# Whole first K load and fewer, larger pieces of the output projection in a decode-attention kernel bound by its load stream

## The chip, the cores and the metric

The kernel runs on one core of a Trainium2 chip. The metric is the device time of one execution in microseconds (us), lower is better. Where I say "span" I mean the time from the first to the last recorded instruction of one execution; it is about 1.4 to 2.0 us shorter than the device time, and it can be compared with positions in the trace.

Engines in the profile: PE is the matmul engine, PEld its weight load, DVE the vector engine, ACT the scalar engine, SP the engine that issues the large loads ("SPq" is its sequencer).

## The reference, cut to what matters

```python
def _A_ref(x, k_cache, v_cache, wq, wo):          # x: one token of 512; 32 heads of 128; 16384 keys
    q = (x @ wq) ...
    scores = jnp.einsum('bhqd,bhkd->bhqk', q, k_cache) * Dh ** (-0.5)
    p = _softmax(scores, axis=-1)
    o = jnp.einsum('bhqk,bhkd->bhqd', p, v_cache)
    return o... @ wo                              # wo: 4096 x 512
...                                               # _B_ref: a small gated MLP
g = _sigmoid((x * gate_w).sum(-1, keepdims=True))
return g * a + (1 - g) * b
```

K and V are 128 MB each in bf16 and are read once. Everything else is small: 4 MB each of `wq` and `wo`, under 3 MB of MLP weights.

## The kernel before

K and V are read in 16 pairs of heads. A load of one pair's K or V is 8 MB: 128 partitions, one row of 64 KB in each. Three such buffers rotate. Loads go out on the SP queue in the order K0, K1, V0, K2, V1, K3 and so on, and each waits until the user of its buffer is done. In particular V1 (the "second V") goes into the buffer of K1, so its issue waits until the scores of pair 1 are finished.

The last load is `wo`, 32 rows of 1 KB per partition, in six pieces. The first 24 rows are multiplied "the wide way" (eight products at a time into four column groups of the array), the rest row by row, two products each.

```python
K_CUTS = (0, 128, 256)
V_CUTS = (0, 160, 224, 256)
WO_CUTS = (0, 16, 24, 28, 30, 31, 32)
WIDE = 24
...
for n, kind, i in loads:
    wait = [user[n - 3]] if n >= 3 else [w_free] if buf[n % 3] is setup else []
    src = (k_src if kind == "k" else v_src)[i]
    cuts, sems = (0, KP), [(ld_k if kind == "k" else ld_v)[i % 2]]
    if n == 0:
        cuts, sems = K_CUTS, ld_kf                    # first K: two halves, two semaphores
    elif i == NP - 1:
        cuts, sems = (K_CUTS, ld_kh) if kind == "k" else (V_CUTS, ld_vp)
    for a, b, done in zip(cuts[:-1], cuts[1:], sems):
        sp.op(lambda e, ...: e.dma_start(out=buf[n % 3][:, a * Dh:b * Dh], ...), wait=..., inc=(done, 16))
...                                                   # (cut)
def warm(e, n, again=False): ...                      # filler products: 128 columns of weights, 512 wide
def fill(e, m): ...                                   # filler product: m columns, no weight load
...                                                   # (cut) the tail, after the last V:
def pe_wide(e):
    va, pa = (counter(e, n, 0) for n in ("wa", "oa"))
    warm(e, 1)
    with e.Fori(0, WIDE // WG) as t:
        ...                                           # eight wide products
        fill(e, 1)
...
w_ok = act.op(lambda e: e.copy(out=d_sb[:, :], in_=d_ps), wait=[(pe.sem, pe.n)], mark=True)
...
for j, (a, b) in enumerate(zip(WO_CUTS[:-1], WO_CUTS[1:])):
    for k in range(max(a, WIDE), b):
        y_ok = add(o2[:, k:k + 1], wo[:, k * D:(k + 1) * D],
                   [(ld_o[j], 16)] if k == a else (), k == H - 1)
    if b == 28:
        add(ones_f[:, 0:1], d_sb[:, :], [w_ok])       # the sums of the wide products
```

The softmax here doesn't subtract the row's maximum and nothing guards it: scores larger than these inputs give would overflow.

## Time and profile before

| | before |
|---|---|
| device time, median of 3 runs | 652.03 us (651.73 to 652.14) |
| span of the profiled execution | 650.5 us |
| bytes loaded | 279.58 MB |
| load queue's share of 16 DMA engines | 99.6% |
| busy PE, DVE, ACT | 66%, 52%, 7% |
| last landing of a `wo` piece (landing records) | 648.53 us |
| from the last landing to the end of the span | 2.00 us |

The first fence is from the page of the profiled execution before. The DMA row has one digit per fortieth of the span, in tenths of busy time (9 is 90% or more). The last line is the chain of waits that ended last.

```profile
span 650.5 us, 7753 instructions
...
PE 428.0 (66%) x2462; PEld 45.7 (7%) x1320; DVE 336.0 (52%) x159; ACT 45.8 (7%) x112; POOL 2.1 (0%) x10
...
DMA  9999999999999999999899999999998999999898
...
q1 hardware_dynamic: 6482, 279.58, 99.6%
...
DMA bufs<-in_A_wo_dram 4%; PE ps_all L719 0%; SPq L645 0%; DVE res L734 0%; ACT p_t L592 0%; ACTq L592 0%; ACTq L612 0%
```

No engine but DMA is near its limit, and the chain ends in the loads of `wo`. So the kernel takes as long as its load stream, plus a short tail.

The next fence is the timeline before, SP and DVE at the start. Columns: start in us, duration in us, engine, line, operation, number of merged instructions, and in brackets how long the engine had been idle and what ended that. L640 on SPq is a K or V load being issued.

```profile
31.83 8.76 DVE L579 TENSOR_TENSOR bufs<-bufs,qb  x2 [0.42 <-DVEq L86]
...
35.27 0.33 SPq L640 DMA_DIRECT2D bufs<-in_A_v_cache_dram  x1
...
59.87 0.33 SPq L640 DMA_DIRECT2D bufs<-in_A_k_cache_dram  x1
...
85.32 0.33 SPq L640 DMA_DIRECT2D bufs<-in_A_v_cache_dram  x1
...
96.69 8.76 DVE L579 TENSOR_TENSOR bufs<-bufs,qb  x2 [12.02 <-DVEq L86]
```

DVE starts on the first K at 31.8 us; V1 is issued at 85.32; DVE waits 12 us for the third K to land at about 96.4.

And the tail before, PE from the last wide group on:

```profile
646.05 0.60 PE L106 MATMUL ps_all<-bufs,o 128*1 x8 [0.72 <-PEq L86]
646.49 0.38 PE L91 MATMUL ps_all<-zero,ident 128*1 128x512 bf16 x1
646.71 0.58 ACT L714 COPY d_sb<-ps_all 128x512 f32<-128x512 f32 x1 [6.01 <-PE ps_all L106]
...
647.20 0.60 PE L719 MATMUL ps_all<-bufs,o 128*1 128x256 bf16 x8 [0.33 <-DMA bufs<-in_A_wo_dram]
...
647.63 0.60 PE L719 MATMUL ps_all<-d_sb,const-float32-1.0 128*1 128x256 f32 x4
...
648.07 0.78 PE L719 MATMUL ps_all<-bufs,o 128*1 128x256 bf16 x8
648.57 0.08 PEld L719 LDWEIGHTS ps_all<-bufs,o 128*1 128x1 bf16 x2 [0.25 <-DMA bufs<-in_A_wo_dram]
648.91 0.36 ACT L734 CAST res<-ps_all 1x256 bf16<-1x256 f32 x1 [1.62 <-PE ps_all L719]
```

The last two weight loads of PE (648.57) wait for a landing, not for PE. The wide sums (the f32 products at 647.63) stand inside the last 1.3 us of PE's work, which ends at 648.89.

### The profile page before, as it was taken

What the parts mean: (1) busy time and instruction counts of PE and PEld (TensorE: products, weight loads), DVE (VectorE), ACT (ScalarE), POOL (GpSimd) and SP (SyncE); (2) the same over time, 40 slices, a digit from 0 to 9 for tenths busy, and PEclk for the clock granted to TensorE, in tenths of its full rate; (3) what the DMA queues carried; (4) which work ended last, traced back from release to release, by engine and by line L of the source; (5) the groups of instructions that cost most, each with busy time, mean ns of one, the idle gap of its engine ahead of it and who ended that gap; (6) DMA issues with size and microseconds to landing.
All of it is one profiled execution on the core that took longest, in us unless ns stands there. A gap on an engine that the chain in (4) does not pass through costs nothing. (4 is left out here: it accounts for less than half of the span.)

```text
span 650.5 us, 7753 instructions
## 1 busy us (share of the span) xinstructions
PE 428.0 (66%) x2462; PEld 45.7 (7%) x1320; DVE 336.0 (52%) x159; ACT 45.8 (7%) x112; POOL 2.1 (0%) x10
## 2 busy tenths in 40 slices
PE   0576866847487574757857476585747757478766
PEld 0000010000101000010000101000010100101012
DVE  3587708356281745618265370835629075465600
ACT  2201010000001000010100001000010100001011
POOL 1000000000000000000000000000000000000000
PEclk9978797969779696987969798686988968798999
DMA  9999999999999999999899999999998999999898
GB/s 387 449 429 451 443 395 451 451 387 451 451 439 399 451 451 415 423 451 451 387 451 451 435 403 451 451 391 447 451 451 387 451 451 431 407 419 484 387 433 342
DMA packets 6491, 279.60 MB, mean 430 GB/s; under 512 B 727, under 2 KB 986, under 8 KB 1370
## 3 DMA queue, kind: packets, MB, share of 16 engines
q1 hardware_dynamic: 6482, 279.58, 99.6%
q8 instruction: 1, 0.02, 0.0%
q10 hardware_dynamic: 8, 0.00, 0.0%
HBM read 279.58 MB, written 0.00 MB: 430 GB/s over the span
## 5 line engine op out<-in xcount | busy, mean ns | idle before, releaser
L579 DVE TENSOR_TENSOR bufs<-bufs,qb x64 | 281.4, 4418 | 168.6 <-DVEq L86 168.6
L91 PE MATMUL ps_all<-bufs,ident 128*128 x960 | 265.0, 432 | 0.0
L496 PE MATMUL ps_all<-bufs,ident 128*128 x64 | 28.4, 444 | 150.8 <-PEq L86 150.8
L106 PE MATMUL ps_all<-bufs,p_t 128*8 x1024 | 79.1, 384 | 30.6 <-PEq L86 19.9
L564 DVE TENSOR_REDUCE s_sb<-ps_all 128x64 f32<-128x512 f32 x64 | 44.0, 688 | 97.4 <-DVEq L86 97.4
L91 PE MATMUL ps_all<-zero,ident 128*8 128x512 bf16 (+1 forms) x147 | 56.4, 384 | 0.0
L592 ACT ACTIVATE p_t<-s_sb 64x256 f32 (+1 forms) x32 | 13.3, 414 | 440.2 <-ACTq L86 439.8
L496 PEld LDWEIGHTS ps_all<-bufs,ident 128*128 128x128 bf16 x64 | 6.3, 99 | 368.0 <-issue 368.0
L106 PEld LDWEIGHTS ps_all<-bufs,p_t 128*8 x1024 | 17.8, 82 | 163.7 <-issue 163.3
L531 PE MATMUL ps_all<-pick,d_sb 128*128 128x2 f32 x128 | 16.8, 253 | 14.8 <-PEq L86 14.8
L531 PEld LDWEIGHTS ps_all<-pick,d_sb 128*128 128x128 f32 x128 | 15.5, 191 | 22.9 <-issue 22.9
L601 ACT COPY d_sb<-ps_all 128x512 f32<-128x512 f32 x16 | 9.4, 585 | 104.3 <-ACTq L86 104.3
L606 ACT CAST ps_all<-zero 128x512 f32<-128x512 bf16 x15 | 8.8, 589 | 1.7
L478 PE MATMUL ps_all<-zero,ident 128*128 128x512 bf16 x18 | 7.0, 389 | 0.0
L669 DVE RECIPROCAL rl<-ps_all 128x32 f32<-128x32 f32 x1 | 0.4, 358 | 11.2 <-PE ps_all L552 11.2
L672 DVE TENSOR_TENSOR o_sb<-ps_all,rl 128x32 bf16<-128x32 f32 x1 | 0.2, 193 | 11.5 <-PE ps_all L531 11.5
L382 DVE TENSOR_TENSOR bufs<-ps_all,ident 128x896 f32<-128x896 f32 x2 | 2.1, 1085 | 7.7 <-PE ps_all L91 7.7
L592 ACT ACTIVATION_READ_ACCUMULATOR p_t<-s_sb (+1 forms) x32 | 5.9, 185 | 0.0
L322 PE MATMUL ps_all<-xgw,const-float32-1.0 1*128 1x3 f32 x2 | 0.6, 358 | 8.0 <-DVE xgw L318 8.0
L106 PE MATMUL ps_all<-bufs,u 128*1 x14 | 2.6, 372 | 3.3 <-ACT ps_all L428 2.5
L91 PE MATMUL ps_all<-bufs,xb 128*128 x12 | 4.4, 491 | 0.0
L346 PE MATMUL ps_all<-bufs,xb 128*128 x4 | 2.1, 517 | 3.2 <-DMA bufs<-in_B_w_in_dram 3.2
(76 smaller groups left out, 42.8 us busy)
## 6 DMA issues: line engine op xcount, KB each, us to landing
bufs<-in_A_k_cache_dram SPq DMA_DIRECT2D x4, 4096.0 KB, 33.2
bufs<-in_A_v_cache_dram SPq DMA_DIRECT2D x1, 5120.0 KB, 33.9
bufs<-in_A_wq_dram SPq DMA_DIRECT2D x1, 4096.0 KB, 12.2
bufs<-in_A_v_cache_dram SPq DMA_DIRECT2D x1, 2048.0 KB, 38.4
bufs<-in_A_wo_dram SPq DMA_DIRECT2D x1, 2048.0 KB, 24.4
bufs<-in_B_w_in_dram SPq DMA_DIRECT2D x1, 1792.0 KB, 15.4
bufs<-in_A_v_cache_dram SPq DMA_DIRECT2D x1, 1024.0 KB, 40.4
bufs<-in_A_wo_dram SPq DMA_DIRECT2D x1, 1024.0 KB, 26.6
```

The source lines that it names most:

```text
L91: ins = eng.matmul(out, lhsT=lhsT, rhs=rhs, **flags).ins
L106: ins = eng.matmul(bank[0:m, 0:n], lhsT=lhsT, rhs=rhs, **flags).ins
L346: if n else matmul_on(nc, e, lambda: e.matmul(args[0], lhsT=args[1], rhs=args[2], **flags), [at, (xa, 0)]))
L382: dve.op(lambda e, h=h, zh=zh: e.tensor_tensor(out=zm[:, 2 * h * ZB:2 * (h + 1) * ZB].rearrange("p (b m k) -> p b m k", b=2, k=FhC), in0=z ...
L478: e.matmul(args[0], lhsT=args[1], rhs=args[2], **flags)
L496: matmul_on(nc, e, lambda: e.matmul(s3, lhsT=ident[:, :], rhs=k3[:, :, 0:W], start=True, **flags), [(kw, 0)])
L531: ins = e.matmul(o2, lhsT=d_sb[:, r * Dh:(r + 1) * Dh], rhs=pick[:, r * 2:(r + 1) * 2], start=False, stop=False, skip_group_check=True)
L564: return e.tensor_reduce(out=s_sb[:, c * QK:(c + 1) * QK], in_=s_ps[c % 2].rearrange("p (j w) -> p j w", w=W), axis=AX.X, op=ALU.add)
L579: e.tensor_tensor(out=k3, in0=k3, in1=qi, op=ALU.mult).then_inc(mul_s, 1)
L592: e.activation(out=p_t[rows, bass.ds(at, NG * 8)].rearrange("p (t c) -> p t c", c=8)[:, :, 4 * s:4 * s + 4], in_=s_sb[rows, :].rearrange(" ...
L601: return e.copy(out=d_sb[:, :], in_=d_ps)
L606: e.copy(out=d_ps, in_=zero[:, :]).then_inc(drn_s, 1)
```

## The change

Its intent: fewer and larger transfers (first K in one load; `wo` in four pieces instead of six), the sums of the wide products moved out of the last microsecond by making only 16 rows wide, and changed filler products on PE.

```diff
-WO_CUTS = (0, 16, 24, 28, 30, 31, 32)
-WIDE = 24
+WO_CUTS = (0, 16, 27, 31, 32)
+WIDE = 16
...
-    ld_kf = [sem(f"ld_kf{b}") for b in range(len(K_CUTS) - 1)]
...
-        warm(e, 2)                       # after each V
+        fill(e, 8, 2)
...
-        if n == 0:
-            cuts, sems = K_CUTS, ld_kf
-        elif i == NP - 1:
+        if i == NP - 1:
...
-        for j in range(len(ld_kf)):
-            hand(e, ld_kf[j], k_s, 1)
+        hand(e, ld_k[0], k_s, 2)
...
-    pe.raw(lambda e: warm(e, 1))         # ahead of the transpose of o
+    pe.raw(lambda e: warm(e, 2))
...
-        warm(e, 1)                       # ahead of the wide products
+        warm(e, 2)
...
+    pe.raw(lambda e: fill(e, 1))
+    add(ones_f[:, 0:1], d_sb[:, :], [w_ok])
     for j, (a, b) in enumerate(zip(WO_CUTS[:-1], WO_CUTS[1:])):
...
-        if b == 28:
-            add(ones_f[:, 0:1], d_sb[:, :], [w_ok])
```

(The rest of the diff only gives `fill` a count and drops an unused argument of `warm`.)

More of the change, by code (lines that the diff above doesn't have):

```diff
@@ L468, in v_buffer, with warm @@
         e.reg_alu(reg, reg, 3, ALU.python_mod)
-    def warm(e, n, again=False):
+    def warm(e, n):
         for j in range(n):
@@ L474, in warm @@
             flags = dict(start=True, stop=True, skip_group_check=True)
-            if j or again:
+            if j:
                 matmul_again(nc, e, *args, **flags)
@@ L478, in warm, with fill @@
                 e.matmul(args[0], lhsT=args[1], rhs=args[2], **flags)
-    def fill(e, m):
-        matmul_again(nc, e, m_ps[0][96:96 + m, :], ident[:, 0:m], zero[:, :], start=True, stop=True,
-                     skip_group_check=True)
+    def fill(e, m, n=1):
+        for _ in range(n):
+            matmul_again(nc, e, m_ps[0][96:96 + m, :], ident[:, 0:m], zero[:, :], start=True,
+                         stop=True, skip_group_check=True)
     def scores(e, i, ka, kw):
```

## The prediction

> **What bounds the kernel.** The load stream. The DMA queue view gives 99.6% of 16 engines' span to queue 1 (279.58 MB). In the transfer records the 16 engines start 1.0 us into the span and never idle until the last piece of the output projection; a 64 KB transfer takes 2.42 us, so 16 engines move 16 x 65,536 B / 2.42 us = 433 GB/s. [...] PE (66%), DVE (52%) and ACT (7%) have slack, and the chain of waits ends in the output-projection loads. So what can change the time is the cost per transfer, and the 2.0 us between the last landing (648.53) and the end (650.5).
>
> **Cost per transfer.** Records by size: 64 KB 2,420 ns, 32 KB 1,213, 16 KB 615, 8 KB 313, 4 KB 160, 2 KB 84, 1 KB 46. A line through the ends gives 37.7 ns per KB plus 8 ns per transfer. Each DMA also writes one semaphore record per engine, 9 ns. An engine carries 8 of the 128 rows.
>
> - First K whole: 8 x (2 x 1,213 - 2,420) + 9 = about 0.06 us saved.
> - Projection pieces: 16, 8, 4, 2, 1, 1 rows cost each engine 8 x (615+313+160+84+46+46) = 10.11 us; 16, 11, 4, 1 cost 8 x (615+423+160+46) = 9.95 us (423 estimated from the line). With two semaphore writes fewer: 0.18 us saved.
>
> The last landing comes 0.24 us earlier, about 648.3.
>
> **First K and DVE.** The halves land at 28.3 and 38.0; DVE starts at 31.8 (held by the gMLP, not by K). Whole, DVE starts at about 38.1, 6.3 us later. The third K then issues at about 66 instead of 59.9, the second V at about 92 instead of 85.3. The stream is queued to about 77 and 97 at those moments, so it never starves. In the timeline DVE idles 12.0 us before the third K (96.7), which absorbs the 6.3. Cost: none.
>
> **The tail on PE.** Wide products of 16 rows take 2 groups of 0.91 us from the landing at 643.3, to about 645.3; ACT copy 0.58, sums 0.36 as today: done by 646.5, before the 11 rows land (about 646.65). The sums thus leave the last microsecond, where they stand today (647.53 to 647.89). Four rows take 0.43 us today, so 11 need 1.18, from 646.7 to 647.9; the next 4 land at about 647.95 and need 0.43, to 648.42; the last row lands at about 648.3. PE thus starts the last two products at 648.42 instead of 648.57: a gain of 0.15 us. The extra filler products only keep PE busy; the granted clock is 1.00 from 636 on (stretches view), and I expect it to stay so.
>
> **Prediction.** 652.03 less 0.15 to 0.24 = 651.85 us. Range 651.4 to 652.3, mostly run-to-run spread (0.4 us among three runs). Faster by over 2%: 0.003; within 2%: 0.994; slower: 0.003.
>
> **What would show it.** DVE's first product at 38; third K issued near 66 with the DMA row still full; sums before the 11 rows; last landing 648.3; the last two products waiting on PE, not on a landing.
>
> **What would make it wrong.** The granted clock falling to 0.5 in the tail: 30 products for 15 rows would take 3.2 us against 1.7 us of landings, up to 1.2 us lost. The stream running dry when the third K or second V issues late: each us is lost whole. More slow transfers (about 0.3 us per engine is lost at 60 to 70 us today) [...]: some tenths either way.

(Two passages are cut: a figure set beside the 433 GB/s that no trace here shows, and a conjecture on what would slow transfers down. Neither was a term of the sum, which came to 0.15 to 0.24 us.)

## The result, and the profile after

A ratio here is the mean time of one kernel's fast runs over that of the other's of the same rounds, so it is not quite the ratio of the medians that are quoted.

The first six runs after: median 652.43 us (651.67 to 652.80), six of before 651.76 (651.71 to 652.14); ratio 1.0007, interval 0.9994 to 1.002: the same. I ran the unedited changed kernel twice more. All 16 runs after, on three occasions: median 652.09, mean 652.13, from 651.62 to 652.80. All 32 fast runs of before: median 651.86, mean 651.91, from 651.66 to 652.42. (One run of before took 957 us and is left out as slow.) In spans: mean 650.52 after (16 runs), 650.43 before (26 runs). So the change gained nothing; if anything it cost 0.1 to 0.2 us (most of that comes from the first six runs; on the two later occasions the means lie 0.05 and 0.14 us above those of before), and its single runs reach 651.4 in span where those of before end at 650.7.

The profiled execution after was one of the fastest. Its page:

```profile
span 650.1 us, 7742 instructions
...
PE 428.8 (66%) x2472; PEld 45.2 (7%) x1312; DVE 336.1 (52%) x159; ACT 45.8 (7%) x112; POOL 2.1 (0%) x10
...
DMA  9999989999999999999999989999998999999898
...
q1 hardware_dynamic: 6050, 279.58, 99.6%
...
PE ps_all L716 0%; PE ps_all L106 0%; PE ps_all L531 0%; PE ps_all L91 0%; PE ps_all L477 0%; ACT d_sb L711 0%; DVE res L731 0%; PE ps_all L677 0%; PE ps_all L673 0%; DVE oT L674 0%
```

432 packets fewer, the same bytes, and the chain that ended last is now made of PE products, no longer of `wo` loads.

The timeline after, SP and DVE at the start:

```profile
34.80 0.33 SPq L638 DMA_DIRECT2D bufs<-in_A_v_cache_dram  x1
38.34 8.76 DVE L579 TENSOR_TENSOR bufs<-bufs,qb  x2 [7.41 <-DVEq L86]
...
66.04 0.33 SPq L638 DMA_DIRECT2D bufs<-in_A_k_cache_dram  x1
...
91.31 0.33 SPq L638 DMA_DIRECT2D bufs<-in_A_v_cache_dram  x1
...
96.39 8.76 DVE L579 TENSOR_TENSOR bufs<-bufs,qb  x2 [5.73 <-DVEq L86]
```

DVE starts 6.5 us later, and so V1 is issued 6.0 us later. DVE still arrives early at the third K (5.7 us of idle time left of 12.0). The tail after:

```profile
645.90 0.60 PE L716 MATMUL ps_all<-d_sb,const-float32-1.0 128*1 128x256 f32 x4 [0.24 <-ACT d_sb L711]
646.45 1.07 PEld L716 LDWEIGHTS ps_all<-bufs,o 128*1 128x1 bf16 x22 [0.46 <-DMA bufs<-in_A_wo_dram]
...
647.75 0.42 PEld L716 LDWEIGHTS ps_all<-bufs,o 128*1 128x1 bf16 x10 [0.23 <-DMA bufs<-in_A_wo_dram]
648.53 0.36 ACT L731 CAST res<-ps_all 1x256 bf16<-1x256 f32 x1 [2.68 <-PE ps_all L716]
```

The sums now stand ahead of the 11 rows. The last 10 weight loads run without a gap after the landing of the 4 rows at 647.71; the last row landed meanwhile, at 647.99. So PE is what ends the tail.

I also worked with three quantities that I computed from the trace's records of single transfers and landings, not from a view of the profile:

- **Work per engine**: the number of transfers of each size times their usual duration (64 KB 2,420 ns, 32 KB 1,213, 16 KB 615, 11 KB 427, and so on), over 16. Before 646.51 us, after 646.31 us: 0.20 us less. This is the forecast's own sum, with the measured 427 ns for an 11 KB transfer where the prediction had estimated 423; it is bookkeeping and not a measurement of time.
- **Last landing**, and the mean of the 16 landings (one per DMA engine) of that last piece.
- **Tail**: span (from the trace, to the nanosecond) minus last landing.

```
kernel       V1 issued  longest extra of   last landing     tail   half-clock stretch
             (us)       a transfer then    last / mean      (us)   after 640 us
                        (94-98.5 us, ns)   of 16 (us)
before        85.32           4            648.53 / 648.38  2.00   none
b_cold        85.64          54            648.47 / 648.13  3.11   644.3 to the end
b_tail        85.97           7            648.15 / 647.90  2.22   642.7 to 646.2
a_khalf       84.81           7            648.17 / 647.92  2.12   none
b_kwhole      91.36         132            648.77 / 648.47  2.00   643.3 to 646.7
after         91.31           8            647.99 / 647.80  2.16   641.0 to 644.4
after_again   90.64           6            647.96 / 647.77  2.09   none
after_third   90.77          11            648.20 / 647.94  2.45   643.6 to 647.0
a_warm        91.21           9            648.22 / 647.84  2.26   643.1 to 646.5
a_cold        91.64         222            648.14 / 647.90  2.96   641.4 to 648.2
a_pieces      91.76         425            648.32 / 647.98  2.00   none
a_hot         92.18        1221            648.69 / 647.90  2.15   none
a_sums        92.28        1338            648.92 / 648.14  2.49   none
a_k32         93.10           6            650.66 / 650.23  2.44   646.0 to 649.4
```

This table holds one traced execution of each kernel (names are explained below; `a_` is an edit of the changed kernel, `b_` of the kernel before). "Longest extra" is how much the slowest 64 KB transfer that began between 94 and 98.5 us took over 2,420 ns; that is where the first transfers of V1 stand (in a_k32, whose stream runs 2.4 us later, they stand 2.4 us later, and there too nothing took over 10 ns longer).

### The profile page after: what moved, and what is told of

Same layout as the page of the kernel before. It is cut to its first block, busy times and chain, and to the rows that moved or that the text cites. A ratio compares the mean times of both kernels' runs of the same rounds, so it can differ in the third digit from the quotient of the medians.

```text
span 650.1 us, 7742 instructions
## 1 busy us (share of the span) xinstructions
PE 428.8 (66%) x2472; PEld 45.2 (7%) x1312; DVE 336.1 (52%) x159; ACT 45.8 (7%) x112; POOL 2.1 (0%) x10
## 3 DMA queue, kind: packets, MB, share of 16 engines
q1 hardware_dynamic: 6050, 279.58, 99.6%
## 5 line engine op out<-in xcount | busy, mean ns | idle before, releaser
L91 PE MATMUL ps_all<-zero,ident 128*8 128x512 bf16 (+1 forms) x165 | 58.2, 385 | 0.0
```

Of the source, the lines that this page charges most:

```text
L91: ins = eng.matmul(out, lhsT=lhsT, rhs=rhs, **flags).ins
```

## The experiments

Theories at the outset. *Clock*: in some executions the array's clock is halved for 3.4 us in the tail, and the change has put more products there. In the clock records of the traces of before and after the granted clock is 1.0 or 0.5 throughout, and the stretches at 0.5 last 3.4 us or more (3.4 to 13.7 us before, 3.4 to 17.1 after). Most half-clock stretches listed above last 3.4 us; that of a_cold lasts 6.8, and that of b_cold from 644.3 us to the end. *Stream*: the whole first K moves DVE's work and disturbs the load stream. *Spread*: there is no difference. Twelve runs, all with five rounds, all correct.

### after_again: the changed kernel unedited

> The changed kernel once more, unedited, for a second trace and five more times. Clock theory (in some executions a 3.4 us half-clock stretch falls on PE's products in the last 6 us, and the change has put more of them there): median 652.2 to 652.6, with single runs spread over 651.6 to 652.9, and whichever profile is slow shows half clock between 644 and 649 us and a gap of over 1 us between last landing and end of the products. Stream theory (the later DVE work after the whole first K makes more slow transfers): same median, but a slow profile shows its last landing after 648.5. Spread theory (no real difference): median within 0.2 of before.

Measured: 652.01 us (651.81 to 652.21) against 651.89 for before on the same chip; ratio 1.0002 (0.9988 to 1.0015). The median is within 0.2 of before's, so this set speaks for *spread*. The profile is a fast one: no half clock from 636.7 us to the end of the products, tail 2.09.

### a_warm: the fillers after each V put back

```diff
-        fill(e, 8, 2)
+        warm(e, 2)
```

> The changed kernel with the two 8-column filler products after each V put back to two 128-column ones. Clock theory, if these fillers are what lets the clock fall in the tail: median near 651.6, spread under 0.5, profile at full clock from 644 to 649. Clock theory, if the fillers do not matter: like the changed kernel, 652.4. Stream theory: like the changed kernel, 652.4.

Measured: 652.25 us (652.00 to 652.70), ratio 1.0006. The profile has a half-clock stretch from 643.1 to 646.5 us although the fillers are the old ones. So the old fillers did not keep the clock up in this trace either. The stretch cost something: the tail is 2.26 us against 2.09 in after_again.

### b_kwhole: before, with only the first K whole

```diff
-    ld_kf = [sem(f"ld_kf{b}") for b in range(len(K_CUTS) - 1)]
...
-        if n == 0:
-            cuts, sems = K_CUTS, ld_kf
-        elif i == NP - 1:
+        if i == NP - 1:
...
-        for j in range(len(ld_kf)):
-            hand(e, ld_kf[j], k_s, 1)
+        hand(e, ld_k[0], k_s, 2)
```

> The kernel before with only the first K made whole. Clock theory: 0.06 us under before, 651.7, spread as before. Stream theory: 652.4 with the wide spread of the changed kernel, and slow transfers in the first 130 us of its trace in place of those at 60 to 90 us.

Measured: 652.07 us (651.84 to 652.19), ratio 1.0001. Neither the 652.4 nor the wide spread of the stream theory. Its trace has several bursts in which most engines' transfers take 0.1 to 0.2 us longer (at 66, 76, 96, 115 and 134 us). The trace of before has such bursts too (66, 86, 144 us), that of a_khalf has none, so they are not the work of the first K. I could not find their cause.

### a_khalf: the changed kernel with the first K in halves

The edit is the reverse of that of b_kwhole, on the changed kernel.

> The changed kernel with the first K in halves again. Clock theory: as the changed kernel, 652.4 with single runs from 651.6 to 652.9. Stream theory: 0.2 us under before, 651.6, narrow spread.

Measured: 651.89 us (651.70 to 652.40), exactly the median of before on that chip; spans 650.3 to 650.6. Not the wide spread that the clock theory asked for, and not a gain of 0.2 us either. Neither theory is settled by these four.

### a_k32: the first K in 32 pieces

```diff
+    ld_kf = [sem(f"ld_kf{b}") for b in range(32)]
...
-        if i == NP - 1:
+        if n == 0:
+            cuts, sems = range(0, KP + 1, KP // 32), ld_kf
+        elif i == NP - 1:
...
-        hand(e, ld_k[0], k_s, 2)
+        for j in range(31):
+            take(e, ld_kf[j], 16)
+        hand(e, ld_kf[31], k_s, 2)
```

> The changed kernel with the first K in 32 pieces of 8 rows, 2 KB per partition. Overhead theory (the stream is busy without a gap, so each transfer's fixed cost goes one to one into the time): 8 x (32 x 84 - 2,420) ns + 31 x 9 ns = 2.4 us on each engine, so last landing near 650.4, span 652.6, time 654.3. Rival (small transfers hide behind something else, so the transfer count does not matter): time as the changed kernel, 652.1, last landing 648.0.

Measured: 654.52 us (654.24 to 654.84), ratio 1.0040 (1.0026 to 1.0054). That is 2.4 us over the 652.09 of the changed kernel, and 2.4 was forecast; the last landing came at 650.66 us, 2.7 us after that of after_again. The landing records show where: K1, the next load after the first K, landed at 59.8 us against 57.4 in after and 57.3 in after_again, and the loads stayed 2.4 to 2.5 us later up to 621 us; the rest of the 2.7 came after that, when the spread of the 16 landings grew from 0.50 to 0.76 us. So more transfers do lengthen the stream, by about the forecast sum, here magnified ten times. The exact hit is partly luck: the 2 KB transfers of this trace took 87 ns in the median and not 84, which would have made the sum 3.2 us.

### a_cold: the changed kernel without fillers in the tail

```diff
-    pe.raw(lambda e: warm(e, 2))
...
-    pe.raw(lambda e: warm(e, 1))
...
-        warm(e, 2)
         with e.Fori(0, WIDE // WG) as t:
...
-            fill(e, 1)
...
-    pe.raw(lambda e: fill(e, 1))
```

> The changed kernel without any filler product after the last V. Clock theory: the granted clock falls to 0.5 in part of 640 to 649 us in most executions, PE ends up to 1.6 us after the last landing instead of 0.47, so time 652.5 to 653.6, with a spread over 0.8. Rival (the tail's clock does not matter, the stream alone sets the end): 652.1, narrow.

Measured: 653.44 us (652.51 to 653.91), ratio 1.0024. The stretches view of a_cold, with one line per stretch of 3 us; after the busy times of PE, PEld, DVE, ACT and POOL come the granted clock, the DMA share and GB/s:

```profile
640.00:643.00 3.00, 1.62 (x13) 1.25 (x13) 0.59 (x3) 0.46 (x1) 0.00 (x0) 0.74 0.94 398
643.00:646.00 3.00, 1.95 (x18) 0.29 (x20) 0.00 (x0) 0.58 (x1) 0.00 (x0) 0.50 0.99 414
646.00:649.00 3.00, 3.00 (x32) 1.70 (x34) 0.00 (x0) 0.00 (x0) 0.00 (x0) 0.63 0.48 182
```

and its timeline in the tail:

```profile
646.78 2.63 PE L712 MATMUL ps_all<-bufs,o 128*1 128x256 bf16 x32
649.48 0.36 ACT L726 CAST res<-ps_all 1x256 bf16<-1x256 f32 x1 [3.56 <-PE ps_all L712]
```

The last landing was at 648.14, no later than usual. The 32 products end 0.95 us later than after (the cast starts at 649.48 against 648.53). So a half clock in the tail does lengthen this kernel, and the time lies in the range that the clock theory gave. This trace is the fastest of the five runs; the slower ones left none.

### b_cold: the kernel before without fillers in the tail

The same edit on the kernel before.

> The kernel before without any filler product after the last V. Clock theory: its last pieces are smaller, 16 products behind the landing at 647.2, so at half clock the end comes at most 0.8 us later: time 652.0 to 652.7, less hurt than the changed kernel's tail without fillers. Rival: 651.9, as before.

Measured: 652.93 us (652.60 to 653.01), ratio 1.0015. The forecast of at most 0.8 us was too small (1.1 us over before's 651.85 of that call): with half clock from 644.3 to the end, its tail took 3.11 us. The forecast order held, for a_cold was 1.6 us over before.

### a_sums: the sums back between the 11 and the 4 rows

```diff
-    add(ones_f[:, 0:1], d_sb[:, :], [w_ok])
     for j, (a, b) in enumerate(zip(WO_CUTS[:-1], WO_CUTS[1:])):
...
+        if b == 27:
+            add(ones_f[:, 0:1], d_sb[:, :], [w_ok])
```

> The changed kernel with the wide sums put back between the 11 rows and the 4 rows. If PE is what ends the changed tail: its last 8 + 2 products start 0.25 to 0.35 us later, products end 0.7 us after the last landing instead of 0.47, span 0.25 us longer. If the last landing ends it: span unchanged, 0.47 us.

Measured: 652.49 us (651.95 to 653.30), spans 650.4 to 651.9. The profile is at full clock in the tail:

```profile
648.58 0.60 PE L716 MATMUL ps_all<-d_sb,const-float32-1.0 128*1 128x256 f32 x4
648.80 0.63 PEld L716 LDWEIGHTS ps_all<-bufs,o 128*1 128x1 bf16 x10
```

The tail is 2.49 us against 2.09 to 2.16, so PE is what ends the changed tail, and moving the sums ahead is worth about 0.35 us in it. But the last landing was also late, at 648.92, and that has nothing to do with the sums. The landing records give two reasons. The 16 landings of a load lay 0.84 us apart from the first K on, more than in any other trace. And V1 was issued late:

```profile
92.28 0.33 SPq L638 DMA_DIRECT2D bufs<-in_A_v_cache_dram  x1
```

At 95.2 to 95.3 us three 64 KB transfers took 0.9 to 1.3 us longer, and the last landing of V1 came 19.90 us after that of the third K, against 19.35 us per load otherwise: 0.55 us lost.

### after_third: the changed kernel once more

> The changed kernel a third time, to pool its times on one more chip with before. If the forecast sum is right (0.15 to 0.24 gained) the mean span is 0.15 to 0.25 under before's of the same call; if something in the change gives it back, the mean span is equal to or above before's. Single runs differ by 0.4 because the skew among the 16 DMA engines, fixed in the first microseconds, differs from run to run: the last landing is later where the spread of the 16 landings of one DMA is wider.

Measured: 652.07 us (651.62 to 652.54) against 651.91 for before (its eight fast runs); ratio 1.0002. Mean span 650.52 against 650.39 for the same eight: something gives the forecast gain back. The last sentence of the expectation was a conjecture. That the skew makes the spread of single runs is not shown, since one run of each set left a trace; that it is fixed early is half right: by 19 us the 16 landings of a load lay 0.40 to 0.84 us apart, depending on the trace, and mostly stayed so; but the spread also changed later, in this trace from 0.67 to 0.57 us near 190 us. The stretches view of this execution, and that of after_again below it:

```profile
640.00:643.00 3.00, 2.77 (x18) 1.43 (x16) 0.60 (x3) 0.53 (x1) 0.00 (x0) 1.00 0.92 389
643.00:646.00 3.00, 2.58 (x19) 0.39 (x16) 0.00 (x0) 0.38 (x1) 0.00 (x0) 0.60 0.98 412
646.00:649.00 3.00, 2.97 (x38) 1.53 (x36) 0.00 (x0) 0.21 (x1) 0.00 (x0) 0.83 0.49 187
```

```profile
640.00:643.00 3.00, 2.62 (x18) 1.28 (x16) 0.59 (x3) 0.25 (x1) 0.00 (x0) 1.00 0.95 403
643.00:646.00 3.00, 2.45 (x23) 0.36 (x20) 0.00 (x0) 0.58 (x1) 0.00 (x0) 1.00 0.96 401
646.00:649.00 3.00, 2.02 (x32) 1.22 (x32) 0.41 (x1) 0.36 (x1) 0.00 (x0) 1.00 0.45 168
```

Same kernel, two executions: granted clock 0.60 and 0.83 in the last two stretches in one, 1.00 in the other. The tail is 2.45 us in the first and 2.09 in the second, and that is most of the difference of their spans (650.7 and 650.1).

### a_hot: the changed kernel with more filler

```diff
-        fill(e, 8, 2)
+        warm(e, 4)
...
-        warm(e, 2)
+        warm(e, 3)
         with e.Fori(0, WIDE // WG) as t:
...
     add(ones_f[:, 0:1], d_sb[:, :], [w_ok])
+    pe.raw(lambda e: warm(e, 2))
```

> The changed kernel with more 128-column filler: four after each V, three ahead of the wide products, two between the sums and the 11 rows. If half-clock stretches in the tail are what gives the forecast gain back: no such stretch after 640 us in the profile, mean span 0.2 to 0.3 under before, spread under 0.5. If skew among the DMA engines alone makes the spread: mean span and spread as the changed kernel's.

Measured: 652.20 us (651.51 to 652.83), ratio 1.0001; spans 650.1 to 651.0. The clock did what was wanted: no half-clock stretch after 635.3 us in the profile, tail 2.15. Yet the spread is as wide as ever, and the profiled execution is a slow one (650.8). So the tail's clock is not the only thing. The issues of a_hot's first loads in the timeline:

```profile
66.63 0.33 SPq L638 DMA_DIRECT2D bufs<-in_A_k_cache_dram  x1
...
92.18 0.33 SPq L638 DMA_DIRECT2D bufs<-in_A_v_cache_dram  x1
...
101.64 0.33 SPq L638 DMA_DIRECT2D bufs<-in_A_k_cache_dram  x1
```

V1 was issued at 92.18, the third K was still landing on the 16 engines between 95.7 and 96.1, and one 64 KB transfer that began at 95.3 us took 3.64 us instead of 2.42. The 16 landings of a load lay 0.45 us apart before that and 1.09 us apart after it. They stayed 1.05 to 1.06 apart through every load to the end, where the last engine landed 0.79 us after the mean (0.19 in the profile of after). So here the skew was not fixed at the start, as the expectation of after_third had it: it was made at V1.

### b_tail: the kernel before with only the tail's cuts

```diff
-WO_CUTS = (0, 16, 24, 28, 30, 31, 32)
-WIDE = 24
+WO_CUTS = (0, 16, 27, 31, 32)
+WIDE = 16
...
+    add(ones_f[:, 0:1], d_sb[:, :], [w_ok])
     for j, (a, b) in enumerate(zip(WO_CUTS[:-1], WO_CUTS[1:])):
...
-        if b == 28:
-            add(ones_f[:, 0:1], d_sb[:, :], [w_ok])
```

> The kernel before with only the projection's cuts, 16 wide rows and the sums first; K in halves and the fillers as before. Forecast sum: work per engine 0.17 us less than before, products end 0.45 to 0.5 us after the last landing (before: 0.36), mean span 0.1 under before. If the missing fillers matter: single spans above 651 and a half-clock stretch after 644 us in some runs.

Measured: 651.88 us (651.78 to 652.26) against 651.91; spans 650.3 to 650.5, none above 651. Work per engine, by the bookkeeping above, 646.37 us, 0.15 less than before (0.17 was forecast). Half clock from 642.7 to 646.2, tail 2.22.

### a_pieces: the changed kernel with the pieces of before

```diff
-WO_CUTS = (0, 16, 27, 31, 32)
+WO_CUTS = (0, 16, 24, 28, 30, 31, 32)
```

> The changed kernel with the pieces of before (16, 8, 4, 2, 1, 1 rows), sums still first and 16 rows wide. Work per engine back up by 0.17 us, but products end 0.36 us after the last landing in place of 0.47, because little is left on PE when the last row lands. Net within 0.1 us of the changed kernel, so the time alone will not tell; the two terms are read from the trace.

Measured: 651.86 us (651.73 to 652.09), ratio 1.0000. Work per engine 646.46 us, 0.15 more than the changed kernel's; tail 2.00 us, 0.09 to 0.16 less than in the traces of merged pieces without a half clock at the end. The two terms cancel, as expected here. The tail of a_pieces:

```profile
648.05 0.08 PEld L716 LDWEIGHTS ps_all<-bufs,o 128*1 128x1 bf16 x2 [0.26 <-DMA bufs<-in_A_wo_dram]
648.36 0.08 PEld L716 LDWEIGHTS ps_all<-bufs,o 128*1 128x1 bf16 x2 [0.22 <-DMA bufs<-in_A_wo_dram]
648.70 0.36 ACT L731 CAST res<-ps_all 1x256 bf16<-1x256 f32 x1 [3.15 <-PE ps_all L716]
```

Its last weight loads wait for a landing again. It is the changed kernel's own piece sizes that put PE behind the last landing.

No version was measurably faster than the kernel before: the best medians, 651.86 to 651.89 of a_pieces, b_tail and a_khalf, lie within 0.1 us of before's.

## Why the prediction was right or wrong

The verdict "same" was right, and so was what bounds the kernel. That verdict was hardly at risk, for all the terms at stake add up to 0.24 us of 652. The number was not good: 651.85 with a top of 652.3 was forecast, and the first six runs had a median of 652.43, 0.13 above that top. The 16 runs together have 652.09, inside the range, but the sign of the small difference is wrong: forecast 0.18 faster, found 0.1 to 0.2 slower, if anything. The signs that the prediction named did appear in the profile after: DVE's first product at 38.34, the third K issued at 66.04, the sums ahead of the 11 rows, the last products waiting on PE.

- **The load stream bounds the kernel: right.** a_k32 adds 2.4 us of transfer overhead by the forecast's sum and costs 2.4 us (its section says what of that is luck). The 64 KB transfers of before give 433 GB/s by their duration of 2.42 us, and its page gives 430 GB/s as the mean over the span.
- **"The last landing comes 0.24 us earlier": by the same bookkeeping with measured durations, 0.20 us.** The last landing is a different thing. It is set by the slowest of 16 engines, which were up to 1.2 us apart in these traces. In the two profiles above it came 0.54 us earlier (648.53 and 647.99), but that is not the change alone: slow transfers cost each engine 0.44 us between 60 and 110 us in the profile before and 0.04 in the profile after. The mean landing moved by 0.58 us, which is close to 0.20 plus these 0.40. In the eleven traces other than a_k32, a_hot and a_sums, the last engine lands 0.15 to 0.38 us after the mean of the 16, so one gain of 0.2 drowns in this.
- **"First K and DVE ... it never starves. Cost: none": this step failed, though not in every execution.** The times in it were right (V1 forecast at about 92, found at 90.6 to 92.3; the stream then queued to about 96), the conclusion was not. I took a load to be ready the moment it is issued. In the traces with whole K a V1 issued up to 91.31 us delayed no first transfer by more than 0.02 us (b_kwhole, at 91.36, shows 0.13, in one of its bursts); at 91.64 the slowest first transfer took 0.22 us longer, at 91.76 0.43, at 92.18 1.22, at 92.28 1.34 us. With the first K in halves V1 goes out at 84.8 to 86.0 and no first transfer took more than 0.06 us longer. When V1 goes out varies by more than a microsecond from run to run and kernel to kernel.
- **What a late V1 cost.** Counted from the issue to the first of the third K's 16 landings the order is the same: no such delay with a lead of 4.31 us or more, b_kwhole's burst apart (in a_k32 the lead was 4.88, although V1 went out at 93.10), 0.22 us at 4.09, 0.43 at 3.80, 1.22 at 3.51, 1.34 at 3.33. That a late issue delays the first transfers is thus supported by a graded series over single traces of different edits; I did not move the issue alone. The delay reached the last landing only in a_hot and a_sums, where V1's came 20.00 and 19.90 us after that of the third K; in a_cold and a_pieces that step was 19.35 and 19.36, as elsewhere, so the delayed engine was not the last one. Three of these edits (a_cold, a_pieces, a_sums) touch only the tail, so together with after, after_again and after_third they are six executions of the changed kernel as far as V1: a first transfer was delayed in three of the six, and the last landing in one. In a_hot and a_sums the delay was not made up by the end: in a_hot the 16 landings of every load after V1 lay 1.05 to 1.06 us apart, and the last engine landed 0.79 us after the mean in a_hot, 0.78 in a_sums. My explanation is an inference: the engines carry equal work (a load of 128 transfers of 2.42 us takes 19.35 us, so eight on each engine), and the stream leaves no gap to catch up (the load queue fills 99.6% of 16 engines' span in before and after). Why a late issue holds up one engine more than the others is not shown.
- The spans point the same way. Leaving out the runs with added cost (a_k32, a_sums, the two cold ones), 7 of 36 runs with a whole first K have a span of 650.8 us or more (a limit that I chose after the fact), up to 651.4; of 36 runs with halves (before, a_khalf, b_tail) none does, the longest being 650.7. Not all seven are V1's: the profile of b_kwhole had bursts of slow transfers instead, and the two longest runs of the changed kernel (651.2 and 651.4) left no trace, so what delayed them stays open.
- **"A gain of 0.15 us" at PE's last products: mis-sized.** I expected PE to be 0.08 us later against the last landing than before. With no half clock after 644.4 us the tail is 2.09 to 2.16 us with the merged pieces (after, after_again, a_khalf, a_hot) and 2.00 with the small ones (before, a_pieces): about 0.13 us. That leaves 0.20 - 0.13 = 0.07 us, and not 0.15 to 0.24.
- **"The granted clock is 1.00 from 636 on, and I expect it to stay so": this failed too.** It held in the one trace of before. In the traces of merged pieces the half-clock stretch that ends at 644.4 cost nothing, one that ends at 646.2 gave a tail of 2.22, at 646.5 2.26, at 647.0 2.45. I had listed this as what would make me wrong ("up to 1.2 us lost"); in these traces it is 0.1 to 0.3 us. The small pieces show 2.00 us with a stretch to 646.7, so they are hurt less by such a stretch, but not by a half clock that lasts to the end (b_cold).

So the forecast gain was small from the start, 0.20 us by count, and PE's own lag of about 0.13 us, seen in each of the four traces of merged pieces without half clock after 644.4 us, takes most of it. A half-clock stretch in the tail and a late V1 each took more in some traces. How much of the measured median each of them makes up is not shown, because only one run of each set left a trace; the 0.07 us that would be left is below what these runs can tell from nothing.

## What to carry to other kernels

When one stream bounds a kernel, fixed cost per transfer (8 ns here, by the line through the 1 KB and 64 KB durations) is worth counting, but a sum of 0.2 us out of 652 is less than the runs of one kernel differ, so no run can confirm it by itself. Also ask of every change upstream by how much it shortens the lead with which later loads are issued; a lead that is positive is not yet enough (here about 4.3 us was, and 3.5 was not), and an engine that falls behind the others can stay behind to the end (in a_hot the 16 landings of a load lay 0.45 us apart before V1 and 1.05 to 1.06 after it). And where the last piece of a stream is merged into larger ones, the compute behind it can become the end, and take a half clock into the time (tail 2.45 us in after_third with a half-clock stretch to 647.0, 2.09 in after_again with none).

## What was measured on the way, and what stays open

- On this core's idle queue in the profile before, the instruction that issued the first load stood at 0.00 to 0.38 us and the first transfer started at 1.00: 0.62 us after the instruction's end. On a full queue, loads issued at 92.18 and 92.28 us (a_hot, a_sums) were late for engines that became free at about 95.3 us, 3 us later; in the traces with an unsplit first K, loads issued at 91.36 or before were not. The lead that a load needs behind a busy stream is not settled.
- In a_hot the spread of the 16 landings of a load stayed at 1.05 to 1.06 us over more than 500 us, after one late transfer had widened it from 0.45.
- The transfers of before from 1 KB (46 ns) to 64 KB (2,420 ns) fit a fixed 8 ns per transfer and 37.7 ns per KB to within 4 ns.
- How much filler keeps the array's clock up is open. Here one or two fillers of 128 columns between the short stages of the tail were not enough in a_warm (half clock from 643.1 to 646.5 us), though the same ones went without a half clock in after_again; none at all gave 6.8 us of half clock in a_cold. No run settles the amount.
